# Words of w_out's tiles in the buffers of the passes' partial results, zeros through TensorE at the start, omega by one transfer

## The chip, the cores and the metric

The kernel runs on one core of a Trainium2 chip. The metric is the device time of one execution in microseconds (us). Below, TensorE is the matmul engine, DVE the vector engine, ACT the scalar engine, and SyncE the engine in whose queue (SPq) most transfers are issued, in order.

## The reference

Three stages follow each other: linear attention with random features, and two feed-forward blocks.

```python
def _attn_ref(q, k, v, omega):        # (4, 8, 576, 64) each; omega (128, 64)
    q_s, k_s = q * scale, k * scale
    def phi(x):
        h = einsum('bhsd,md->bhsm', x, omega) - sum(x * x) / 2
        return exp(h - max(h)) / sqrt(m)
    kv  = einsum('bhsm,bhsd->bhmd', phi(k_s), v)
    num = einsum('bhsm,bhmd->bhsd', phi(q_s), kv)
    return num / (phi(q_s) . sum_s phi(k_s) + 1e-6)

def _moe_ref(x, w_a, w_b, w_out):     # x (2304, 512), w_a and w_b (512, 1536), w_out (1536, 512)
    return (x @ w_a * (x @ w_b)) @ w_out

def _moe2_ref(x, w_in, w_out):        # w_in (512, 2048), w_out (2048, 512)
    h = maximum(x @ w_in, 0)
    return (h * h) @ w_out
```

The weights are 64-bit floats in memory. The kernel reads them as pairs of 32-bit words.

## The kernel before, in words

Every 64-bit weight is turned into a sum of two reduced-precision parts, high and low. `load` brings the words of one or two 128x512 pieces into a buffer named `raw` (two buffers of 8 KB per partition); `split` makes the two parts: ACT reads the upper words into `a` (L211), DVE puts the bits together in `p` in three steps (L212, L216, L220; L220 is the last reader of the words), ACT casts the high part (L226), and DVE subtracts for the low part (L227). A tile of w_a and one of w_b share a `raw` buffer (L194); a tile of w_out takes one for itself (L190).

The prologue loads omega twice (L365, L366), side by side, transposes it on TensorE (L375), and ACT writes it as OMS, OM and OMZ. The first head pair of k is loaded (L441), transposed (L465), copied to S on ACT (L468), projected with OMZ in full precision (`phi_wide`, L415), reduced on DVE for the minimum (L419) and put through the exponential on ACT (L421). The last 64 rows of all heads, the tail, go the same way in `kt_steps` after a transpose of their own (`tail_turn`, L403). Products of k's features with v are `ps_kv` (L571) and `ps_kt` (L539).

The first feed-forward block runs in passes over one block of 256 tokens (passes 0 to 5) or two (later ones). A pass of the first six covers half the hidden dimension, six tiles f; for every f there are the gate matmuls `ab` (L786) with w_a and w_b, and two units later the matmuls `y` (L811) with w_out in `outs`. Passes 0 and 1 (f 0 to 5) make w_out's tiles 0 to 5 new; passes 2 and 3 (f 6 to 11) the tiles 6 to 11. A made tile is stored as `wo_d` and loaded again later (L1597). At the end of a pass the sums in PSUM go to a tile of `ypool`: in passes 0, 1 and 4 as `y_s` (ACT, L846), then to memory (L847); in passes 2, 3 and 5 the earlier half is loaded as `y_p` (`prefetch`, L976) and added (DVE, L840). `ypool` has two buffers of 2 KB per partition with the tag `ys`; in the first 40 us they hold V2, the v of odd head pairs. Attention lanes for later batches (`SIDES`) are laid between the units. The order on each engine and queue is fixed when the program is built.

The units and their splits are driven by `load_split`, which issues a load, and by `step`, which counts units down until the split is laid out. `tc.issue_after(x)` makes the instructions of its block come after x on x's engine.

Of the kernel before, what the change touches and what calls it, by code (L numbers as in the profile page):

```python
# [8 lines left out]
F32 = mybir.dt.float32  # L9
# [35 lines left out]
def kernel(  # L45
# [13 lines left out]
    nc = tc.nc  # L59
# [122 lines left out]

    def load(*parts):


        raw = top["raw"].tile([128, 2, 512, 2], I32, tag="raw", name="raw")
# [13 lines left out]
    def split(raw, t, behind=None, apart=False, put_off=None):  # L200
# [3 lines left out]
        n = raw.shape[1]  # L204
# [3 lines left out]
        for x in (slice(0, 1), slice(1, 2)) if apart else (slice(0, n),):  # L208
            a, p, r, o = a_[:, x], p_[:, x], raw[:, x], t[:, x]
            with tc.issue_after(behind.ins) if behind else nullcontext():  # L210
                nc.scalar.activation(out=a, in_=f32(r[:, :, :, 1]), func=ACTF.Copy, scale=WORD_SCALE)  # L211
# [8 lines left out]
            nc.vector.scalar_tensor_tensor(  # L220
                out=p.bitcast(U32), in0=r[:, :, :, 0].bitcast(U32), scalar=29,
                in1=p.bitcast(U32), op0=ALU.logical_shift_right, op1=ALU.bitwise_or,
            )
# [18 lines left out]
    later_parts, later_n = [], [9]  # L242
# [114 lines left out]

    def prologue():
# [49 lines left out]
    def phi_wide(rows, dst):  # L408
# [5 lines left out]
        for x, s in enumerate(rows):  # L414
            state["proj"] = nc.tensor.matmul(  # L415
                ps[:, 2 * x:2 * x + 2].rearrange("p h m -> p (h m)"), lhsT=s,
                rhs=OMZ.rearrange("p h m -> p (h m)"), start=True, stop=True,
            )
# [7 lines left out]
    class Side:  # L426
# [28 lines left out]
        def t1_main(self):  # L455
# [60 lines left out]
    def kt_steps(b, g):  # L516
# [11 lines left out]
        st = tail_turn("k", b, g)  # L528
# [246 lines left out]
    def a_units():  # L775
# [26 lines left out]
        def outs(pi, f):  # L802
# [26 lines left out]
            if wide:  # L829
                for c in range(KC):  # L830
                    t = ypool.tile([128, 2, N], F32, tag="ys", name="y_s")
# [5 lines left out]
            for c in range(0, KC, 2):  # L837
# [6 lines left out]
                else:  # L844
                    t = ypool.tile([128, 2, N], F32, tag="ys", name="y_s")
# [125 lines left out]
        def prefetch(pi, f):  # L971
            bl, f0, f1 = PASSES[pi]
            if f0 and f == f1 - 1:
                for c in range(0, KC, 2):
                    part[pi, c] = ypool.tile([128, 2, N], F32, tag="ys", name="y_p")
# [814 lines left out]
```

## Time and profile before

| | |
|---|---|
| Time, median of 3 runs (lowest to highest) | 978.43 us (976.73 to 978.84) |
| Profiled execution, its own time | 979.28 us |
| Its span in the trace | 977.2 us |
| TensorE busy (share of the span) | 961.5 us (98%) |
| DVE busy | 728.8 us (75%) |
| ACT busy | 551.5 us (56%) |
| Chain of work that ended last | TensorE 81%, DVE 7%, transfers 5%, ACT 4% |

The span runs from the first instruction to the last; the profiled execution's own time has 2.1 us more around it. Busy time counts an engine as busy while any of its instructions is under way. Matmuls overlap each other in the pipeline, so the time from one start to the next says more of their rate than their duration does. A full-precision matmul of 256 columns shows as two records.

### The profile page before, as it was taken

To read this page: it belongs to the slowest core of one execution; us is meant where nothing else is said; L and a number is where in the kernel's file an instruction comes from. 1 tells how busy PE (TensorE), PEld (TensorE's weight loads), DVE (VectorE), ACT (ScalarE), POOL (GpSimd) and SP (SyncE) were. 2 spreads that over 40 slices of the span, in tenths; PEclk is the share of its full clock that TensorE was granted. 3 is DMA by queue.
4 is the path that set the end of the run, shared out by engine and by line. 5 is a ranking of instruction groups with operands and counts; after the bars stand their busy time and mean duration, and the time that the engine had idled before them with its cause. 6 is when DMAs were issued, how large, how long until landed. Compare 5 with 4: busy or idle time off the path is not lost.

```text
span 977.2 us, 18208 instructions
## 1 busy us (share of the span) xinstructions
PE 961.5 (98%) x6625; PEld 898.0 (92%) x6625; DVE 728.8 (75%) x1688; ACT 551.5 (56%) x1310; POOL 28.8 (3%) x54
## 2 busy tenths in 40 slices
PE   7999999999999999999999999999999999999998
PEld 6799998999998889889998888899999999999998
DVE  3888689887787865565456989789787347988794
ACT  5876566666655643253433544677676565555561
POOL 4000100000000000000000000000000000000000
PEclk9999999999999999999999999999999999999999
DMA  8656976655775365346547989246666869944301
GB/s 207 208 176 204 307 234 212 226 179 182 218 213 167 130 199 171 113 153 188 170 143 254 350 304 339 66 160 207 216 227 220 317 250 357 390 135 146 115 17 50
DMA packets 121961, 198.39 MB, mean 203 GB/s; under 512 B 28944, under 2 KB 84752, under 8 KB 119440
## 3 DMA queue, kind: packets, MB, share of 16 engines
q1 hardware_dynamic: 120336, 195.65, 60.5%
q0 software_dynamic: 1536, 1.58, 0.6%
q8 instruction: 53, 0.87, 0.4%
q14 instruction: 36, 0.29, 0.1%
HBM read 136.90 MB, written 60.29 MB: 202 GB/s over the span
## 4 chain that ended last, share of the span: by engine, by line
PE 81%; DVE 7%; DMA 5%; ACT 4%; issue 2%; SPq 0%; DVEq 0%; ACTq 0%
PE y L811 13%; PE abw L786 9%; PE oY L1478 8%; PE pY L1294 7%; PE ab L786 7%; PE oX L1478 5%; PE oW L1478 5%; PE sP L919 5%; PE pW L1294 4%; PE sR L919 3%; PE ps_n L638 3%; PE ps_kv L571 3%; PE ps_p L415 3%; PE ps_p L490 2%; DMA raw<-in_moe_w_b_dram 2%; PE ps_qt L628 2%
## 5 line engine op out<-in xcount | busy, mean ns | idle before, releaser
L786 PE MATMUL abw<-x_all,W 128*128 128x512 f32 x432 | 104.1, 392 | 0.0
L786 PEld LDWEIGHTS abw<-x_all,W 128*128 128x128 f32 x432 | 80.0, 188 | 15.7
L786 PE MATMUL ab<-x_all,W 128*128 128x256 f32 x576 | 84.9, 290 | 0.4 <-ACT W L226 0.4
L786 PEld LDWEIGHTS ab<-x_all,W 128*128 128x128 f32 x576 | 74.0, 189 | 1.7 <-ACT W L226 0.6
L811 PE MATMUL y<-g_mid,wo 128*128 128x512 f32 x288 | 75.1, 401 | 0.0
L811 PE MATMUL y<-gs,wo 128*128 128x256 f32 x432 | 66.5, 290 | 0.0
L811 PEld LDWEIGHTS y<-g_mid,wo 128*128 128x128 f32 x288 | 51.9, 188 | 10.1
L811 PEld LDWEIGHTS y<-gs,wo 128*128 128x128 f32 x432 | 56.6, 189 | 1.0 <-DVE wo L227 0.2
L1294 PE MATMUL pY<-W,M 128*128 128x384 f32 x228 | 44.1, 336 | 0.4 <-ACT F L1312 0.4
L499 ACT COPY c<-ps_p 128x256 f32<-128x256 f32 x76 | 27.7, 372 | 28.6 <-PE ps_p L490 28.1
L501 DVE CUSTOM_DVE_ANT_0 c<-ps_p,c 128x128 f32<-128x128 f32 x152 | 38.2, 285 | 7.5 <-ACT c L499 6.8
L786 PE MATMUL ab<-x,W 128*128 128x256 f32 x288 | 42.5, 288 | 0.0
L1442 ACT CAST W<-F 128x384 fp32r<-128x384 f32 x57 | 29.1, 513 | 22.9 <-PE oX L1478 11.0
L1478 PE MATMUL oX<-W 128*128 128x256 f32 x351 | 41.9, 276 | 0.0
L1478 PEld LDWEIGHTS oX<-W 128*128 128x128 f32 x351 | 40.8, 188 | 0.0
L1294 PEld LDWEIGHTS pY<-W,M 128*128 128x128 f32 x228 | 39.8, 188 | 1.0 <-ACT F L1312 0.9
L1320 ACT ACTIVATE F<-F 128x384 f32<-128x384 f32 x48 | 24.7, 518 | 26.9 <-DVE F L1315 26.7
L1478 PE MATMUL oY<-W 128*128 128x256 f32 x315 | 38.6, 277 | 0.0
L786 PEld LDWEIGHTS ab<-x,W 128*128 128x128 f32 x288 | 37.6, 191 | 0.1
L506 ACT ACTIVATE qp<-c,nm 128x128 f32<-128x128 f32 x88 | 31.0, 397 | 11.3 <-DVE nm L501 10.8
L1478 PEld LDWEIGHTS oY<-W 128*128 128x128 f32 x315 | 37.1, 188 | 0.0
L419 DVE TENSOR_REDUCE nm<-ps_p 128x4 f32<-128x512 f32 (+1 forms) x44 | 24.7, 564 | 14.9 <-PE ps_p L415 14.7
(287 smaller groups left out, 2408.7 us busy)
## 6 DMA issues: line engine op xcount, KB each, us to landing
wo<-wo_d SPq DMA_DIRECT2D x60, 512.0 KB, 3.9
s_d<-F SPq DMA_DIRECT2D x24, 768.0 KB, 4.7
tsum<-t_d SPq DMA_DIRECT2D x26, 512.0 KB, 4.0
t_d<-cut SPq DMA_DIRECT2D x40, 256.0 KB, 2.9
raw<-in_moe_w_out_dram SPq DMA_DIRECT2D x32, 256.0 KB, 5.2
raw<-in_moe_w_in_dram SPq DMA_DIRECT2D x16, 512.0 KB, 6.4
raw<-in_moe_w_a_dram SPq DMA_DIRECT2D x12, 512.0 KB, 3.8
raw<-in_moe_w_b_dram SPq DMA_DIRECT2D x12, 512.0 KB, 5.8
```

The source lines that it names most:

```text
L415: state["proj"] = nc.tensor.matmul(ps[:, 2 * x:2 * x + 2].rearrange("p h m -> p (h m)"), lhsT=s, rhs=OMZ.rearrange("p h m -> p (h m)"), st ...
L499: nc.scalar.copy(out=c, in_=ps[:, :, 1, :])
L501: nc.vector.tensor_tensor_reduce(out=c[:, x, :], in0=ps[:, x, 0, :], in1=c[:, x, :], scale=1.0, scalar=3.0e38, op0=ALU.add, op1=ALU.min, a ...
L506: nc.scalar.activation(out=dst[:, 2 * n + x, :], in_=c[:, x, :], func=ACTF.Exp, scale=-1.0, bias=nm[:, x:x + 1],)
L571: lambda h=h, j=j: nc.tensor.matmul(ps[:, h, :], lhsT=kp[:, 4 * h + j, :], rhs=V2[h][:, j] if odd else V[:, j, h, :], start=(j == j0), sto ...
L638: lambda x=x: nc.tensor.matmul(pn[:, x, :], lhsT=t["qT"][:, x % 2 * len(g) + x // 2, :], rhs=kv[:, x % 2, :], start=True, stop=True,)
L786: nc.tensor.matmul(ps, lhsT=wv[:, s_, kc, :], rhs=x[..., kc, m_, :], start=(kc == 0 and (s_, m_) == TERMS[0]), stop=(kc == KC - 1 and (s_, ...
L811: nc.tensor.matmul(y_part(pi, f, c), lhsT=wo[pi, f][:, s_, c * 128:(c + 1) * 128], rhs=g[:, m_, :],  start=(f == f0 and (wide or c % 2 == ...
L919: nc.tensor.matmul(ps[:, z], lhsT=b(z, s_, kk), rhs=a[:, kk, m_, :], start=(first and z == 0 and kk == 0 and (s_, m_) == TERMS[0]), stop=( ...
L1294: nc.tensor.matmul(ps[c][:, x, 0:TH], lhsT=w[:, s_, 128 * kk:128 * kk + 128], rhs=y[:, ai, kk, m_, :], start=((c, x) not in seen and kk == ...
L1442: ahead_of["cast"] = nc.scalar.copy(out=sop[:, 0], in_=src)
L1478: nc.tensor.matmul(tiles_of(p, t), lhsT=sops[n][:, s_, 128 * t:128 * t + 128], rhs=w[:, m_, :], start=(fresh and k == 0 and (t % 2 == 0 or ...
```

## The change

Three things are changed. First, from w_out's third tile on (`O_APART = 2`) `load` puts the words into two tiles of `ypool` with the tag `ys`, 512 words each, by two transfers, and `split` reads them in two halves, on ACT (L211 before) and in the last of the three DVE steps (L220 before). `y_stage`, by which the passes' results now get their tiles, first lays out the splits of all such tiles that are still waiting.

Second, a region of W that is not yet in use is filled with zeros, copied from OMZ, which is cleared first; V and VT are cleared after that. TensorE multiplies these zeros into a bank that nobody reads: 8 matmuls ahead of omega's transpose, 6 after it, and 4 after the transposes of the first tile of k. The first projections stand behind the last of them, and the tail's transpose behind the projections.

Third, omega comes by one transfer that reads it twice. The laying out of the first tile's parts also moves by one step (`later_n`, 9 to 10).

```diff
+    def y_stage(name):
+        while any(x[1][0] == "o" and x[1][1] >= O_APART for x in waiting):
+            split_next()
+        return ypool.tile([128, 2, N], F32, tag="ys", name=name)
     def load(*parts):
+        if parts[0][2] and parts[0][1] >= O_APART:
+            w, f, _ = parts[0]
+            raws = []
+            for z in range(2):
+                t = ypool.tile([128, 2, N], F32, tag="ys", name="rawo").rearrange("p a n -> p (a n)")
+                nc.sync.dma_start(
+                    out=i32(t), in_=w[f * 128:(f + 1) * 128, 512 * z:512 * z + 512]
+                )
+                raws.append(i32(t).rearrange("p (f w) -> p f w", w=2))
+            return raws
...
             with tc.issue_after(behind.ins) if behind else nullcontext():
-                nc.scalar.activation(out=a, in_=f32(r[:, :, :, 1]), func=ACTF.Copy, scale=WORD_SCALE)
+                for a_x, _, r in pieces:
+                    nc.scalar.activation(
+                        out=a_x, in_=f32(r[..., 1]), func=ACTF.Copy, scale=WORD_SCALE
+                    )
...
-    later_parts, later_n = [], [9]
+    later_parts, later_n = [], [10]
...
+    zero = area["W"][:, FA * 2048 - 256:FA * 2048]
+    blank = bank(7, [128, 512], "blank")[:, 0:256]
+    def fill(n):
+        for _ in range(n):
+            state["fill"] = nc.tensor.matmul(
+                blank, lhsT=zero[:, 0:128], rhs=zero, start=True, stop=True,
+            )
...
-        nc.sync.dma_start(out=om[:, 0, :], in_=omega)
-        nc.sync.dma_start(out=om[:, 1, :], in_=omega)
-        nc.vector.memset(V, 1.0)
-        nc.vector.memset(VT, 1.0)
+        nc.sync.dma_start(out=om, in_=omega.unsqueeze(1).to_broadcast([M, 2, D]))
+        nc.vector.memset(OMZ, 0.0)
+        t = nc.vector.tensor_copy(out=zero, in_=OMZ.rearrange("p a m -> p (a m)"))
+        with tc.issue_after(t.ins):
+            t = nc.vector.memset(V, 1.0)
+        with tc.issue_after(t.ins):
+            nc.vector.memset(VT, 1.0)
...
-        nc.vector.memset(OMZ, 0.0)
+        fill(8)
         ps = at_bank([128, M], "ps_om")
-        nc.tensor.transpose(ps, om.rearrange("p a d -> p (a d)"), ident)
+        with tc.issue_after(state["fill"].ins):
+            t = nc.tensor.transpose(ps, om.rearrange("p a d -> p (a d)"), ident)
+        with tc.issue_after(t.ins):
+            fill(6)
...
+        with tc.issue_after(state["fill"].ins) if "proj" not in state else nullcontext():
             for x, s in enumerate(rows):
                 state["proj"] = nc.tensor.matmul(
...
+            elif "k" in self.at:
+                with tc.issue_after(state["fill"].ins):
+                    for c in cols:
+                        t = nc.tensor.transpose(ps[:, c], nat[:, c], ident)
+                with tc.issue_after(t.ins):
+                    fill(4)
...
         yield
-        st = tail_turn("k", b, g)
+        if state["n"] < 4:
+            yield
+            with tc.issue_after(state["proj"].ins):
+                st = tail_turn("k", b, g)
+        else:
+            st = tail_turn("k", b, g)
```

The four places that took `ypool.tile(..., tag="ys", ...)` for `y_s` and `y_p` call `y_stage` instead, the one in the wide passes too.

## Rows read from the trace of the kernel before

**Rows 1.** The page: busy us (share of the span) and instructions

```profile
PE 961.5 (98%) x6625; PEld 898.0 (92%) x6625; DVE 728.8 (75%) x1688; ACT 551.5 (56%) x1310; POOL 28.8 (3%) x54
```

**Rows 2.** Waits of TensorE, whole run: us in total, times, longest us

```profile
PE ps_om L375 <- DMA om<-in_omega_dram: 3.0, 1, 3.0
```

**Rows 3.** Timeline of TensorE, 0 to 16: start us, us, engine, line, names, count

```profile
5.00 1.11 PE L465 MATMUL ps_t<-ident,kn 128*128 128x128 f32 x4 [1.54 <-DMA kn<-in_k_dram]
6.79 1.22 PE L415 MATMUL ps_p<-OMZ,S 128*128 128x256 f32 x2 [0.68 <-ACT S L468]
...
8.02 2.77 PE L415 MATMUL ps_p<-OMZ,S 128*128 128x256 f32 x6
10.58 1.06 PE L415 MATMUL ps_p<-OMZ,T 128*128 128x256 f32 x2
...
12.28 0.42 PE L463 MATMUL ps_t<-ident,qn 128*128 128x128 f32 x1
...
12.82 0.30 PE L465 MATMUL ps_t<-ident,kn 128*128 128x128 f32 x1
...
15.00 1.35 PE L415 MATMUL ps_p<-OMZ,S 128*128 128x256 f32 x5
```

**Rows 4.** Busy us of PE, PEld, DVE, ACT, POOL; clock, DMA; 40 to 180

```profile
40.00:180.00 140.00, 137.67 (x1077) 130.54 (x1076) 117.74 (x260) 91.42 (x233) 9.34 (x16) 1.00 0.72 231
```

**Rows 5.** Waits of SyncE's queue, 40 to 180; landing of L190's loads

```profile
SPq L190 <- DVE p L220: 24.2, 7, 5.7
SPq L194 <- DVE p L220: 18.4, 8, 4.5
...
DMA to landing us min/median/max: 3.4/3.9/7.7
```

**Rows 6.** Timeline of DVE, 0 to 13

```profile
0.95 0.49 DVE L369 MEMSET V<- 128x520 f32 x1
...
1.99 0.27 DVE L373 MEMSET OMZ<- 128x256 f32 x1
...
9.11 0.69 DVE L419 TENSOR_REDUCE nm<-ps_p 128x4 f32<-128x512 f32 x1 [4.25 <-PE ps_p L415]
```

**Rows 7.** Groups by form, ACT, then DVE: count | busy us, mean ns

```profile
L211 ACT ACTIVATE a<-raw 128x512 f32<-128x512 f32 x16 | 10.9, 680 | 8.6 <-DVE den L612 2.7 <-DMA raw<-in_moe_w_b_dram 2.4 <-DVE den L609 1.6
...
L1065 DVE TENSOR_TENSOR gs<-a_s,gs 128x256 fp32r<-128x256 f32 x36 | 15.1, 419 | 1.6 <-ACT gs L1065 1.2
...
L220 DVE SCALAR_TENSOR_TENSOR p<-raw,p 128x512 uint32<-128x512 uint32 x16 | 10.9, 686 | 0.2
```

**Rows 8.** Timeline of SyncE's queue, 0 to 6

```profile
1.19 0.42 SPq L366 DMA_DIRECT2D om<-in_omega_dram  x1
1.65 0.43 SPq L441 DMA_DIRECT2D kn<-in_k_dram  x1
2.13 0.77 SPq L561 DMA_DIRECT2D V<-in_v_dram  x1
```

**Rows 9.** Timeline of TensorE, from 118 on

```profile
119.51 2.99 PE L786 MATMUL ab<-x_all,W 128*128 128x256 f32 x24
```

**Rows 10.** Timeline of ACT, 0 to 15

```profile
11.54 1.14 ACT L421 ACTIVATE kp<-ps_p,nm 128x128 f32<-128x128 f32 x4 [0.57 <-DVE nm L419]
...
14.57 0.87 ACT L468 COPY S<-ps_t 128x256 f32<-128x256 f32 x2
```

**Rows 11.** Timeline of SyncE's queue, 118 to 182

```profile
137.17 1.44 SPq L847 DMA_DIRECT2D y_d<-y_s  x2
...
140.06 0.85 SPq L190 DMA_DIRECT2D raw<-in_moe_w_out_dram  x1
143.69 0.93 SPq L976 DMA_DIRECT2D y_p<-y_d  x2
```

**Rows 12.** Timeline of DVE, 120 to 180

```profile
133.85 0.68 DVE L220 SCALAR_TENSOR_TENSOR p<-raw,p 128x512 uint32<-128x512 uint32 x1
...
173.64 1.29 DVE L840 SCALAR_TENSOR_TENSOR y_p<-y,y_p 128x512 f32<-128x512 f32 x2
```

More of the change, by code (lines that the diff above doesn't have):

```diff
@@ L200, in split @@
     def split(raw, t, behind=None, apart=False, put_off=None):
-        n = raw.shape[1]
+        halves = None
+        if isinstance(raw, list):
+            halves = [(slice(256 * z, 256 * z + 256), r) for z, r in enumerate(raw)]
+        n = 1 if halves else raw.shape[1]
         a_, p_ = (
@@ L208, in split @@
         for x in (slice(0, 1), slice(1, 2)) if apart else (slice(0, n),):
-            a, p, r, o = a_[:, x], p_[:, x], raw[:, x], t[:, x]
+            a, p, o = a_[:, x], p_[:, x], t[:, x]
+            if halves:
+                pieces = [(a[:, 0, c], p[:, 0, c], r) for c, r in halves]
+            else:
+                pieces = [(a, p, raw[:, x])]
             with tc.issue_after(behind.ins) if behind else nullcontext():
-                nc.scalar.activation(out=a, in_=f32(r[:, :, :, 1]), func=ACTF.Copy, scale=WORD_SCALE)
+                for a_x, _, r in pieces:
+                    nc.scalar.activation(
+                        out=a_x, in_=f32(r[..., 1]), func=ACTF.Copy, scale=WORD_SCALE
+                    )
             nc.vector.tensor_scalar(
@@ L219, in split @@
             )
[L220 to L223, printed above, removed]
+            for _, p_x, r in pieces:
+                nc.vector.scalar_tensor_tensor(
+                    out=p_x.bitcast(U32), in0=r[..., 0].bitcast(U32), scalar=29,
+                    in1=p_x.bitcast(U32), op0=ALU.logical_shift_right, op1=ALU.bitwise_or,
+                )
             def parts(o=o, p=p):
@@ L413, in phi_wide @@
         ps = at_bank([128, n, M], "ps_p")
[L414 to L418, printed above, removed]
+        with tc.issue_after(state["fill"].ins) if "proj" not in state else nullcontext():
+            for x, s in enumerate(rows):
+                state["proj"] = nc.tensor.matmul(
+                    ps[:, 2 * x:2 * x + 2].rearrange("p h m -> p (h m)"), lhsT=s,
+                    rhs=OMZ.rearrange("p h m -> p (h m)"), start=True, stop=True,
+                )
         nc.vector.tensor_reduce(out=nm, in_=ps, axis=AXX, op=ALU.min)
@@ L830, in outs @@
                 for c in range(KC):
-                    t = ypool.tile([128, 2, N], F32, tag="ys", name="y_s")
+                    t = y_stage("y_s")
                     nc.scalar.mul(out=t, in_=yp[pi][c], mul=Y_SCALE)
@@ L844, in outs @@
                 else:
-                    t = ypool.tile([128, 2, N], F32, tag="ys", name="y_s")
+                    t = y_stage("y_s")
                     nc.scalar.mul(out=t, in_=yp[pi][c // 2], mul=Y_SCALE)
@@ L974, in prefetch @@
                 for c in range(0, KC, 2):
-                    part[pi, c] = ypool.tile([128, 2, N], F32, tag="ys", name="y_p")
+                    part[pi, c] = y_stage("y_p")
                     nc.sync.dma_start(out=part[pi, c], in_=y_cols(bl[0])[:, c:c + 2, :])
```

3 lines of the change are left out of this document (added).

## The prediction

> **What bounds the kernel now.** I read the page's busy shares first: TensorE is busy 98% of the span [rows 1], so nothing but an idle or a slow stretch of TensorE can be won, and any stall put into its in-order queue is paid in full. Next the list of what TensorE waited for: its two longest waits of the whole run are both in the first 5 us, 3.0 us for omega and 1.5 us for the first tile of k [rows 2, 3]. Then the timeline of its first 15 us [rows 3]. What to see there is not only the gaps but the spacing: six records of the projection `ps_p` start at 8.02 and the next form starts at 10.58, 0.427 us a record; the five from 15.00 on last 1.35 us together, some 0.24 a record (less the drain of the last). So TensorE runs at half its rate (1.2 instead of 2.4 GHz) until about 12.8: a transpose's duration is 0.42 at 12.28 and 0.30 at 12.82 [rows 3]. The granted clock of the page shows full rate there; I go by the spacing. Before the rise the engine had worked since 6.79, from 8.02 on without any break.
>
> For the middle of the kernel I read one window and one list. In the 140 us from 40 to 180, in which all the w_out splits that the change touches lie (the first two excepted), TensorE is idle for only 140.00 - 137.67 = 2.33 us, beside DVE at 84% [rows 4]. In the same stretch SyncE's queue stands 24.2 and 18.4 us for a `raw` buffer, that is for the last DVE operation of an earlier split [rows 5]. The queue waits; TensorE hardly does.
>
> **The start, step by step.** OMZ is cleared first, then copied to the zeros. The memset is 0.27 us and starts at 0.95 in the place of V's [rows 6]; the trace has no such copy, so I take between 0.27 (that memset) and 0.42 (a DVE operation of the same 128x256 on two inputs [rows 7]). The zeros stand at about 1.6. V's memset then ends at some 2.1 instead of 1.44, and V's load is behind it in SyncE's queue: it was issued at 2.13 [rows 8], so it keeps its place, and all loads behind it keep theirs.
>
> Omega by one transfer takes one issue of 0.42 us out of the queue, and the load of k behind it moves from 1.65 to about 1.2 [rows 8]. Its price as one issue is not in the trace; twice as many runs as one of the two halves, so between 0.42 and the 0.77 of V's load. Gain for k: 0 to 0.45 us.
>
> The 18 fills are 128x256 matmuls. Twenty-four of that form take 2.99 us at full rate, 0.12 us each [rows 9]; at half rate 0.24. Eight run from 1.6 to 3.5, omega's transpose follows (it waited until 3.02 before), six more end at about 5.2, then come the four transposes of k, which began at 5.00. While the clock is low the fills thus take the whole gain of the earlier k, and cost up to 0.3 us; four more behind the transposes cover S's copy (done just before 6.79 [rows 3]) and end about when it does. TensorE is at work without a break from 1.6.
>
> When does the clock rise? The one rise of this trace came 4.8 to 6.0 us after the work became unbroken (from 8.02, or from 6.79 if a first short break is not counted, to 12.8) [rows 3]. The same distance from 1.6 gives 6.4 to 7.6; I take 7.1, just as `ps_p` starts. Then the chain is: first four records at half of 0.427 each and 0.16 of drain, done at 8.1 (the reduce started at 9.11 [rows 6]); reduce 0.69, then four exponentials 1.14: 9.95. The other four records end at 9.1, their exponentials wait for ACT and end at 11.1 (before: 11.54 + 1.14 = 12.68 [rows 10]). The remaining products of k and v are some 0.9 us at full rate, so S is copied at 12.3 instead of 14.57, and the next projections start at 12.7 instead of 15.00: 2.3 us saved. TensorE would save 2.9 at full rate (13 records and transposes, 0.21 each); ACT's chain of exponentials keeps 0.6 of it. If the clock rises at 6, the sum is 2.7; at 8.5, about 1.2; never earlier than now, 0.3 lost. From 15 on the work is bound by TensorE, ACT and DVE, not by times of arrival, so I carry 2.3 us to the end.
>
> On the clock the Trainium skill, "TensorE: Matmul & The Clock Gate", section "Part 4: PE-mode transpose", says that transposes do not count as busy TensorE in the way that matmuls do. The kernel before cannot decide it: its only early transposes are followed by a gap. By that rule the zeros fall into pieces with transposes between, which is the second rival below. The tail's transpose of k is also put behind the first projections; it stood between two of them and cost the first reduce one record, 0.21 us at half rate, and that is in the sum above.
>
> **The places of w_out.** For ten of the twelve splits the words go to the two `ys` buffers instead of half a `raw` buffer. Each costs one more issue (0.34 us on SyncE), and two halves on DVE: 2 x 0.42 instead of 0.69 [rows 7], 0.15 us, so 1.5 us of DVE in 140, beside TensorE's work. ACT's own pass over the words is cut in two likewise, at most the same 0.15 each. I cost this at nothing: DVE has 22 us of idle in the stretch [rows 4], and if that cover were gone it would be 1.5.
>
> What it gives: w_a's and w_b's pairs no longer queue behind w_out's words, up to 24.2 + 18.4 us of SyncE's waits [rows 5]. For TensorE that is worth at most its idle 2.33 us.
>
> What it adds: both `ys` buffers make one tile of w_out, so from one such load to the next nothing overlaps: the next is issued only when the last DVE operation of the split before has read both halves, and the partial results of the passes stand in the same two buffers. The worst place is pass 2, where six w_out tiles, two stores of y and two loads of y_p meet. Before, load 8 was issued at 140.06 while the stores of y were still under way, and y_p was loaded at 143.69, thirty us ahead of its use at 173.64 [rows 11, 12]. After, load 8 waits for the stores to land and y_p for the last split. One turn is the load's 3.9 us [rows 5], ACT's 0.7 [rows 7] and the three DVE operations with what stands between them, some 2.5: 7.1. Tile 6 has its words read by 134.5 as before [rows 12], 7 by about 141; y is evicted behind that and stored until about 148 (before, store and landing took from 137.17 to at most 143.69 [rows 11]), then 8, 9, 10 and 11 at 155, 162, 169 and 176, and y_p lands at 180. The eviction that ends the pass came at 173.64 [rows 12], so the w_out lane would end the pass some 6 us late, 3 if a turn is 6.3. Queued behind these waits on SyncE are loads of q and k and the reloads of w_out. TensorE has other work then: gate matmuls of two units (each 2.99 [rows 9]) and the attention lanes. I take the lateness as covered to most of its length and set gain against loss: 0, with -2.3 and +7 as the ends.
>
> The sum: -2.3 + 0. From the profiled execution's 979.28 (span 977.2 and 2.1 around it) that is 977.0; that execution stood 0.85 above the median of 978.43, so I forecast 976.1, with 974.8 to 977.3 as its own range from the clock's rise at 6 or at 8.5.
>
> **Rivals.**
> The raw buffers pay. With w_a and w_b earlier, the idle of 40 to 180 goes: 976.1 - 2.3 = 973.8. For: the queue's 42 us of waits. Against: DVE, at 84%, takes the splits no faster.
>
> The clock does not rise earlier (the zeros, or the transposes among them, count for less than the rows suggest): 0.3 us late instead of 2.3 early, 978.7. Against: the one rise in the trace followed work that also had transposes in it, as at 12.28 [rows 3].
>
> The ys buffers become the bound, and it is slower than before. The place is pass 2 and the start of pass 3; y's matmuls of pass 3 need the banks that the eviction with y_p frees, due at 173.64. It decides as soon as that eviction is later than the work at hand covers: the two gate units are 6.0 us if they are still free to run, nothing if their own buffers wait for the same y. 180 against 173.64 is 6.4; I take 5: 976.1 + 5 = 981.1. For: single buffering where there were two. Against: TensorE's idle of 2.33 us shows that the order laid out at build time finds other work.
>
> **How the numbers follow.** Chances: forecast 0.45, raw buffers pay 0.22, no earlier rise 0.17, ys the bound 0.16. A measurement of this kernel tells about 0.2% from no change, 1.96 us, so faster means under 976.5 and slower over 980.4. Of the forecast 0.32 lies below 976.5; with 0.21 of the first rival and 0.01 of the second, faster is 0.54. Slower is 0.14 of the last rival and 0.02 of the second, 0.16. The rest, 0.30, is the same. The range reaches down to 973.4 (both gains, 2.7 and 2.3, off 978.4) and up to 980.6 (the lower half of the last rival).
>
> **What would show it.** The start is right if the spacing of `ps_p` falls to 0.22 before 8 us and the projections of 15.00 come at about 12.7; wrong if records at 0.43 still stand at 10. The single omega shows in k's issue at 1.2. The ys lane shows in SyncE's waits: those of w_a and w_b for a raw buffer shrink, and loads of w_out stand for the split before or for y's store. If TensorE's idle in the stretch of passes 2 and 3 grows by more than 2 us, the last rival holds. The forecast fails if the build lays out the attention lanes in another order, which no row here can show.

## The result and the profile after

The changed kernel takes **982.33 us** (median of 7 runs, 981.45 to 985.5) against 977.96 for the kernel before (7 runs, 975.95 to 979.28): a ratio of **1.0053, interval 1.0038 to 1.0069**. It is slower by 0.4 to 0.7%, above the range of 973.4 to 980.6. The profiled execution has a span of 980.1 us.

In every fence below, the line numbers are those of the changed kernel: L461 is the projection (L415 before), L843 the gate matmuls (L786), L199 a load of w_out's words into a `ys` buffer (`rawo`), L212 a load of w_a's or w_b's pair, L249 the DVE operation that reads a split's words last.

The page, busy us and share of the span, and the same window as [rows 4] (busy us of PE, PEld, DVE, ACT, POOL; clock, DMA):

```profile
PE 963.6 (98%) x6643; PEld 899.0 (92%) x6643; DVE 730.1 (74%) x1699; ACT 553.8 (57%) x1320; POOL 29.0 (3%) x54
```

```profile
40.00:180.00 140.00, 136.79 (x1066) 129.37 (x1065) 114.00 (x261) 90.87 (x236) 9.44 (x16) 1.00 0.64 211
```

TensorE is still the bound. Between 40 and 180 us it idles 3.2 us where it idled 2.3 [rows 4], with eleven matmuls fewer done in the stretch.

**The start** is better than forecast in this execution. TensorE's timeline of the first 18 us, after (start us, us, engine, line, names, count, idle before):

```profile
1.55 2.07 PE L393 MATMUL blank<-W 128*128 128x256 f32 x8 [1.55 <-DVE W L408]
3.42 0.41 PE L418 MATMUL ps_om<-ident,om 128*128 128x128 f32 x1
...
4.92 0.64 PE L513 MATMUL ps_t<-ident,kn 128*128 128x128 f32 x4
...
6.23 1.13 PE L461 MATMUL ps_p<-OMZ,S 128*128 128x256 f32 x4 [0.20 <-ACT S L520]
...
7.30 1.03 PE L461 MATMUL ps_p<-OMZ,S 128*128 128x256 f32 x4
...
11.59 2.42 PE L461 MATMUL ps_p<-OMZ,S 128*128 128x256 f32 x10
...
16.97 0.63 PE L517 MATMUL ps_t<-ident,kn 128*128 128x128 f32 x4 [0.80 <-DMA kn<-in_k_dram]
```

Four transposes of k take 0.64 us where they took 1.11, and four projections 1.13 where six took 2.77 [rows 3]: TensorE is at 2.4 GHz by 4.9 us, where before it was by 12.8. (The granted clock of the profile reads 1.00 in all of these stretches, before and after, so this goes by durations and spacing, as in the prediction.) The next projections start at 11.59 instead of 15.00. But then the four transposes at 16.97 stand 0.80 us for a tile of k: the start has caught up with its loads.

The clock does not rise as early in every execution with these 18 zeros. In yp_pool, a run below with the same start, the first four projections take 1.50 us in place of 1.13, so the rise falls among them, and the next projections come 0.8 us later than in the change:

```profile
6.66 1.50 PE L461 MATMUL ps_p<-OMZ,S 128*128 128x256 f32 x4
...
12.39 2.43 PE L461 MATMUL ps_p<-OMZ,S 128*128 128x256 f32 x10
```

**Pass 2** runs much as laid down in the prediction. SyncE's queue from 118 us on (`x2` are the two halves of a tile; the `x3` are the second half of tile 8 and both of tile 9), and the eviction with y_p on DVE:

```profile
133.04 0.82 SPq L199 DMA_DIRECT2D rawo<-in_moe_w_out_dram  x2
...
145.41 6.24 SPq L199 DMA_DIRECT2D rawo<-in_moe_w_out_dram  x3
...
161.46 0.80 SPq L199 DMA_DIRECT2D rawo<-in_moe_w_out_dram  x2
...
168.60 0.80 SPq L199 DMA_DIRECT2D rawo<-in_moe_w_out_dram  x2
...
175.02 0.89 SPq L1033 DMA_DIRECT2D y_p<-y_d  x2
176.00 0.42 SPq L1654 DMA_DIRECT2D wo<-wo_d  x1
```

```profile
178.45 0.69 DVE L897 SCALAR_TENSOR_TENSOR y_p<-y,y_p 128x512 f32<-128x512 f32 x1
```

From 161.46 to 168.60 is one turn of the single pair of buffers, 7.14 us. y_p is loaded at 175.02 instead of 143.69 [rows 11], and the eviction of the pass begins at 178.45 instead of 173.64 [rows 12], 4.8 us late. Behind y_p's wait in SyncE's queue stands the reload of w_out for pass 3, issued at 176.00. TensorE's waits from 140 to 190 us (us in total, times, longest), and SyncE's from 40 to 180:

```profile
PE y L868 <- DMA wo<-wo_d: 1.4, 1, 1.4
PE ps_xt L763 <- DVE xh L670: 0.9, 1, 0.9
PE ps_p L461 <- ACT T L450: 0.6, 1, 0.6
PE ps_nt L751 <- ACT qT L747: 0.5, 1, 0.5
```

```profile
SPq L199 <- DVE p L249: 25.3, 8, 4.9
SPq L212 <- DVE p L249: 21.4, 6, 7.1
```

The four waits of TensorE are the stretch's whole idle time, 3.4 us. Before, the same stretch had 1.1 us of it:

```profile
140.00:190.00 50.00, 48.94 (x389) 46.05 (x389) 43.65 (x127) 32.71 (x87) 3.51 (x6) 1.00 0.74 243
```

It has thus grown by 2.3 us. More than 2 us of it in passes 2 and 3 was the prediction's sign for its last rival. SyncE's two waits for a buffer, which the change might have been thought to end, are 25.3 and 21.4 us instead of 24.2 and 18.4 [rows 5]: they did not shrink.

### The profile page after: what moved, and what is told of

It reads as the page before. It is cut to its first block, busy times and chain, and to the rows that moved or that the text cites. A ratio compares the mean times of both kernels' runs of the same rounds, so it can differ in the third digit from the quotient of the medians.

```text
span 980.1 us, 18274 instructions
## 1 busy us (share of the span) xinstructions
PE 963.6 (98%) x6643; PEld 899.0 (92%) x6643; DVE 730.1 (74%) x1699; ACT 553.8 (57%) x1320; POOL 29.0 (3%) x54
## 4 chain that ended last, share of the span: by engine, by line
PE 82%; DVE 6%; DMA 5%; ACT 3%; issue 1%; SPq 1%; DVEq 0%; ACTq 0%
PE y L868 14%; PE abw L843 9%; PE pY L1351 8%; PE ab L843 8%; PE oY L1535 7%; PE oX L1535 5%; PE sP L976 5%; PE oW L1535 4%; PE pW L1351 4%; PE sR L976 3%; PE ps_n L695 3%; PE ps_kv L628 2%; DMA t_d<-cut 2%; PE pX L1351 2%; PE ps_p L461 2%; PE ps_p L542 2%
## 5 line engine op out<-in xcount | busy, mean ns | idle before, releaser
L843 PE MATMUL abw<-x_all,W 128*128 128x512 f32 x432 | 104.2, 392 | 0.0
L843 PEld LDWEIGHTS abw<-x_all,W 128*128 128x128 f32 x432 | 80.0, 188 | 15.8
L843 PE MATMUL ab<-x_all,W 128*128 128x256 f32 x576 | 84.1, 289 | 0.0
L843 PEld LDWEIGHTS ab<-x_all,W 128*128 128x128 f32 x576 | 73.7, 189 | 0.9 <-ACT W L255 0.2
L843 PE MATMUL ab<-x,W 128*128 128x256 f32 x288 | 43.5, 289 | 0.0
L843 PEld LDWEIGHTS ab<-x,W 128*128 128x128 f32 x288 | 37.9, 190 | 0.0
L558 ACT ACTIVATE qp<-c,nm 128x128 f32<-128x128 f32 x88 | 30.9, 397 | 11.3 <-DVE nm L553 10.5
L695 PEld LDWEIGHTS ps_n<-kvr,qT 128*128 128x128 f32 x256 | 32.0, 191 | 4.1 <-ACT qT L690 2.4
```

The costliest lines, as they stand in the source:

```text
L558: nc.scalar.activation(out=dst[:, 2 * n + x, :], in_=c[:, x, :], func=ACTF.Exp, scale=-1.0, bias=nm[:, x:x + 1],)
L695: lambda x=x: nc.tensor.matmul(pn[:, x, :], lhsT=t["qT"][:, x % 2 * len(g) + x // 2, :], rhs=kv[:, x % 2, :], start=True, stop=True,)
L843: nc.tensor.matmul(ps, lhsT=wv[:, s_, kc, :], rhs=x[..., kc, m_, :], start=(kc == 0 and (s_, m_) == TERMS[0]), stop=(kc == KC - 1 and (s_, ...
```

## The experiments

Theory S at the outset: the start gains and w_out's places cost, and both add. Its rival, R, put the loss on the order of the lanes that the moved start brings with it. Later runs ask what of the places costs, and where the start's gain goes. All medians are given beside the kernel before on the same chip.

### One half of the change at a time

start_only keeps the change's start, with w_out as before:

```diff
-    O_APART = 2
+    O_APART = 99
```

> The changed kernel without its new places for w_out: the words of all tiles go to the raw buffers, as before; zeros, single omega transfer and order of the start are kept. Theory S (the start wins what the trace of the changed kernel shows at 20 us, 2.4, and the w_out places lose all the rest): faster than before by 2.4, that is about 975.5, ratio 0.9975. Rival R (the moved start makes the build lay out the later lanes in another order, and it is that order that loses between 200 and 280): 978 to 980, ratio 1.000 to 1.002.

Measured: 977.4 (11 runs) against 977.85, 0.9998 [0.9989, 1.0007]. Neither expectation is met. The premise of rival R fails too: from 40 to 300 us all of TensorE's 1996 matmuls stand in the order of the kernel before. start_again is the same kernel once more.

> The start alone once more, for a second profile. At 15 us it should lead by about 3 again (the clock rises near 4.8). If the loss of 2.8 between 240 and 285 is of its nature, it comes again; if it is chance, it is smaller or elsewhere.

Measured: 978.33, and a span of 976.2, as in the first. The start alone is thus worth 0.4 us and not distinguishable from nothing, though its projections stand at 12.02 and 11.52 in the two, instead of 15.00 [rows 3]. before_again is the kernel before once more.

> The kernel before once more, for a second profile. It tells how much of a lag between two profiles is chance. If the stretch from 240 to 285 was lucky in the first profile (stores of t_d landing early), this one lags it there by 1 to 3 us; if the shifted start loses there by its nature, this one agrees with the first within 0.3.

Measured: 976.77, span 974.9. It corrects a number that the prediction rests on: in this execution the projections of [rows 3] come at 14.00, not 15.00. The transposes ahead of them take 0.28 us each from 11.27 on, so the clock had risen by then, against 12.8 in the first profile. So 1.0 of the 3.4 us between [rows 3] and the profile after is a late start of the kernel before. On the stretch from 240 to 285 us it agrees with the first profile to about 0.3 us (its matmuls compared with the first profile's, one by one in order). start_only loses 3.0 us there against that profile, start_again 1.7: a loss that comes again, though not in full.

ys_only has the places, and the start as before:

```diff
-        nc.sync.dma_start(out=om, in_=omega.unsqueeze(1).to_broadcast([M, 2, D]))
+        nc.sync.dma_start(out=om[:, 0, :], in_=omega)
+        nc.sync.dma_start(out=om[:, 1, :], in_=omega)
...
-        fill(8)
...
-            fill(6)
...
```

(the rest of the start goes back in the same way, `later_n` too)

> The kernel before with the new places for w_out alone; the start is that of before. Theory S: slower than before by 4.4 + 2.4 = 6.8, about 984.7, ratio 1.007, and the lag against before grows at 75 to 95, 140 to 185 and 200 to 280. Rival R: slower by no more than what is lost up to 185, about 4, ratio 1.004, with no further loss between 200 and 280.

Measured: 985.03, 1.0074 [1.0061, 1.0086]: 7.2 us slower, as theory S had it. **The places are the loss.**

### Which tiles

early_four uses the places for tiles 2 to 5, late_six for 6 to 11 (which meet the stores of y and y_p in pass 2); the start is the change's in both:

```diff
-    O_APART = 2
+    O_APART = range(2, 6)
```

(in the two comparisons, `in` for `>=`), and

```diff
-    O_APART = 2
+    O_APART = 6
```

> The changed kernel with the new places for w_out's tiles 2 to 5 alone (pass 0); tiles 6 to 11 stay in the raw buffers, so y's stores and the loads of y_p share their buffers with nothing. Theory S: only the loss of 75 to 95 stays: 975.5 + 1.9 = 977.4, ratio 0.9995. Rival: if the loss between 200 and 280 stays too, about 980.

> The changed kernel with the new places for w_out's tiles 6 to 11 alone (passes 1 and 2); tiles 2 to 5 stay in the raw buffers. Theory S: the loss of 75 to 95 (1.6 to 2.2) is gone and the losses of passes 2 and 3 and after stay: about 980.5, ratio 1.0025. Rival: if the loss is that of the early tiles, about 977.

Measured: early_four 980.79, 1.0029 [1.0019, 1.0038]; late_six 981.89, 1.0045 [1.0031, 1.006]; both beside start_only's 977.4. The four early tiles cost 3.4 us, the six late ones 4.5, together more than the whole change's 4.9. Theory S had 1.9 for the early tiles and missed; early_four's time is near that of its rival, about 980. Busy time in two stretches, as in [rows 4], of start_only, early_four and late_six in turn:

```profile
75.00:100.00 25.00, 24.96 (x204) 24.28 (x203) 21.47 (x49) 16.49 (x42) 3.54 (x7) 1.00 0.66 219
...
140.00:190.00 50.00, 49.11 (x393) 46.45 (x392) 43.92 (x128) 31.98 (x85) 3.50 (x6) 1.00 0.75 244
```

```profile
75.00:100.00 25.00, 24.24 (x187) 23.00 (x188) 21.14 (x51) 15.07 (x39) 3.39 (x6) 1.00 0.64 212
...
140.00:190.00 50.00, 47.77 (x378) 44.88 (x377) 43.28 (x126) 32.64 (x87) 3.51 (x6) 1.00 0.74 240
```

```profile
75.00:100.00 25.00, 24.96 (x200) 24.17 (x199) 21.64 (x47) 16.41 (x40) 2.33 (x4) 1.00 0.69 237
...
140.00:190.00 50.00, 46.55 (x360) 43.14 (x361) 42.34 (x127) 31.46 (x88) 3.49 (x6) 1.00 0.57 189
```

TensorE's idle from 75 to 100 us, where no partial result stands in the way, goes from 0.04 to 0.76 us with the early tiles and not with the late ones. From 140 to 190 the late tiles take it from 0.9 to 3.45, as much as the whole change shows there; the early ones to 2.2. The number of matmuls done tells the same: 189 and 365 in the whole change, 204 and 393 in start_only.

### Queues

yp_pool issues y_p's two loads from GpSimd's queue, so that the reload of w_out does not stand behind them:

```diff
-                    nc.sync.dma_start(out=part[pi, c], in_=y_cols(bl[0])[:, c:c + 2, :])
+                    nc.gpsimd.dma_start(out=part[pi, c], in_=y_cols(bl[0])[:, c:c + 2, :])
```

> The changed kernel with the loads of y_p issued from GpSimd's queue instead of SyncE's. Theory (the reload of w_out for pass 3 stands in SyncE's queue behind the loads of y_p, which wait for the last split): the wait of y for that reload, 1.4 us near 180, goes, the time falls by about that, to 981. Rival (it is y_p itself, late, that holds the eviction and so the banks): the wait moves to the eviction, and the time stays at 982.3.

Measured: 982.65, 1.0047 [1.0028, 1.0065]: both expected times lie in the interval. TensorE's wait of 1.4 us for the reload is gone; what stands in its place, from 165 to 190 us, is

```profile
PE y L868 <- DVE y_p L897: 0.4, 1, 0.4
```

The time is not told apart from the change's: 1 us less in one wait is inside the interval. pool_queue moves the words of w_out to GpSimd's queue as well:

```diff
-                nc.sync.dma_start(
+                nc.gpsimd.dma_start(
                     out=i32(t), in_=w[f * 128:(f + 1) * 128, 512 * z:512 * z + 512]
```

> The whole change, with the loads of w_out's words into the ys buffers and the loads of y_p issued from GpSimd's queue, so that nothing on SyncE's queue stands behind a wait for a ys buffer. If what the places cost is what stands behind these waits on SyncE (loads of q and k, the reload of wo), most of the 5 us between after and start_only goes: 977.5 to 979.5. If it is the order in which the lanes stand on the engines, and the single pair of buffers itself, the time stays at 981 to 983.

Measured: 990.62, 1.0129 [1.0108, 1.015], far above both expectations. GpSimd's queue carries the tails of k, q and v, and these now stand behind the waits (40 to 190 us):

```profile
POOL rawo L199 <- DVE p L249: 29.2, 3, 10.6
POOL rawo L199 <- DVE xh L670: 25.4, 1, 25.4
```

So the waiting was not lifted by another queue, only moved to one with other work in it. By which of these waits it became 8 us worse was not followed further.

### The places or the halves

halves_in_raw takes away the places, and with them `y_stage`'s early laying out of the waiting splits, which no run tells apart from the places. The words still come in two loads and are read in two halves by ACT and DVE, but they lie in a half of a `raw` buffer, and the partial results have the `ys` buffers for themselves. The start is the change's.

```diff
-        while any(x[1][0] == "o" and x[1][1] >= O_APART for x in waiting):
-            split_next()
...
+            raw = top["raw"].tile([128, 2, 512, 2], I32, tag="raw", name="raw")
...
-                t = ypool.tile([128, 2, N], F32, tag="ys", name="rawo").rearrange("p a n -> p (a n)")
+                t = raw[:, 0, 256 * z:256 * z + 256]
...
```

> The whole change but the places: w_out's tiles from the third on are loaded in two halves and read in two halves by ACT and DVE as in after, but the words stay in half a raw buffer, and the partial results of the passes have the ys buffers for themselves as in before. The start is after's, with 18 fills. If the single pair of buffers is what costs (each load waits for the split before, for y's stores, and y_p for the last split), this runs as start_only does, 977.4, plus at most the 1.5 us of DVE: 977.4 to 978.9. If the halves and the other order in which the lanes then stand on the engines are the cost, it runs as after: 981 to 983.

Measured: 976.9 (12 runs), 0.9989 [0.9977, 1.0002]: 5.4 us below the change, near the expectation of the single pair (977.4 to 978.9). Another order of the lanes comes with the halves too: of start_only's 1996 matmuls between 40 and 300 us, 1752 are found in the same order in this kernel, 1754 in early_four, 1802 in late_six and 1723 in the change. early_four and late_six, whose order is no newer than this one, lose 3.4 and 4.5 us; this one loses nothing. It isn't the very order of the change. halves_again is the same kernel once more.

> One more look at halves_in_raw. Its first profile showed TensorE at a wait of 1.3 us for the third tile of k at 17 us and a granted clock of 0.85 and 0.50 in the two stretches of 5 us from 15. If that belongs to the early start of this kernel it comes again; if it belongs to that execution, the granted clock stays 1.00 and the span is some 974.5.

Measured: 976.73, span 975.0. Busy time by stage, of the change and then of halves_again:

```profile
75.00:100.00 25.00, 24.24 (x189) 22.87 (x188) 21.18 (x50) 16.01 (x41) 3.12 (x6) 1.00 0.63 217
140.00:190.00 50.00, 46.60 (x365) 43.49 (x364) 42.71 (x127) 31.75 (x90) 3.01 (x6) 1.00 0.55 186
190.00:260.00 70.00, 68.45 (x556) 65.18 (x555) 56.51 (x212) 46.07 (x140) 3.99 (x7) 1.00 0.63 192
```

```profile
75.00:100.00 25.00, 24.95 (x200) 23.83 (x199) 21.77 (x51) 16.87 (x44) 2.92 (x6) 1.00 0.70 227
140.00:190.00 50.00, 48.34 (x385) 45.80 (x384) 44.15 (x131) 32.07 (x89) 3.49 (x6) 1.00 0.73 239
190.00:260.00 70.00, 69.77 (x575) 67.15 (x574) 59.06 (x229) 48.69 (x154) 3.49 (x6) 1.00 0.64 195
```

Idle time of TensorE is 0.76, 3.40 and 1.55 us against 0.05, 1.66 and 0.23, so 3.8 of the 5.1 us between the two spans. DVE, ACT and the DMA engines do less in the change's stretches too: none of them has become the bound. And w_a's and w_b's loads, which were to be freed, wait less where w_out stays beside them: 17.7 us in halves_again from 40 to 190, 21.4 in the change.

### How many zeros

three_fills is start_only with one zero product in each of the three places, 3 instead of 18:

```diff
-        fill(8)
+        fill(1)
...
-            fill(6)
+            fill(1)
...
-                    fill(4)
+                    fill(1)
```

> The start alone with three zero matmuls in all (one at each place) instead of eighteen; order and single omega transfer kept. Theory (the unbroken work of the zeros brings the clock's rise forward): the rise falls back to about 12, and the lead at 15 us falls from 3.0 to 0.4 or less. Rival (the earlier k and the moved tail's transpose make most of the lead): the lead stays at 2 or more.

> The same kernel as three_fills, beside three_short on the same chip: 975.7 (975.0 to 976.4) again. A profile that loses over 1 us behind 20 us against the first one would say that such losses belong to an execution and not to the kernel.

Measured: three_fills 975.71 (10 runs), **0.9982 [0.9970, 0.9994]**, and three_again, the same kernel, 976.13 (12 runs), 0.9984 [0.9973, 0.9996]. Both are faster than the kernel before, with a later rise of the clock than the change has. TensorE's first microseconds:

```profile
6.18 2.04 PE L461 MATMUL ps_p<-OMZ,S 128*128 128x256 f32 x4 [0.46 <-ACT S L520]
...
8.18 1.03 PE L461 MATMUL ps_p<-OMZ,S 128*128 128x256 f32 x4
...
12.45 2.42 PE L461 MATMUL ps_p<-OMZ,S 128*128 128x256 f32 x10
```

The rise falls between the first four projections and the next, at about 8 us, and the projections of 11.59 come at 12.45; in three_again they come at 13.15. So the lead over [rows 3] stayed near 2 us (2.6 and 1.9), as the rival had it, but the clock rose well ahead of the 12 us of the theory. No run has the new order of the start without any zeros, so what the three zeros give of these 2 us, and what the earlier k and the single transfer of omega, is not told apart.

three_again also lost more behind 20 us than three_fills did: its span is 2.6 us longer, and 0.7 of that is the start. By its own expectation such losses belong to an execution. A single wait of one profile is to be read with that in mind.

Compared with start_only, all other instructions stand in the same order on every engine. start_only's projections come at 12.02 (11.52 in start_again), 0.4 to 0.9 us ahead of three_fills, and its median is 1.7 behind. Its start leads TensorE to the third tile of k before it has landed, and there the lead ends: the transposes of that tile stand at 16.84 in start_only, 16.83 in start_again and 16.87 in three_fills. Behind that start_only loses more. Theory F for this loss: 15 products and 15 weight loads more move each later fetch of TensorE's instructions against the work, onto transfers that the lanes wait for. Three kernels vary the number and the work apart. short_fills has 18 fills of 8 columns:

```diff
-                blank, lhsT=zero[:, 0:128], rhs=zero, start=True, stop=True,
+                blank[:, 0:8], lhsT=zero[:, 0:128], rhs=zero[:, 0:8], start=True, stop=True,
```

> The start alone with its 18 fills, but each of 8 columns instead of 256: as many instructions on TensorE as in start_only, hardly any of their work. start_only (18 fills) ran 977.4, three_fills 975.7, and the two differ in nothing but 15 zero products ahead of the first projections. Theory F, the fetches of TensorE's instructions: 15 products and their 15 weight loads more move each later fetch to an earlier place in the work, where it falls beside stores of t_d and a load of w_b that the attention lanes wait for. Then the number of instructions counts, not their work: TensorE loses 0.8 us at 55 to 63 and over 1 us each near 246 and 267, as in start_only, and the time is 977.4 (976.7 to 978.1). Rival C, the early rise of the clock itself sets the lanes against their transfers: with fills this short the clock rises as late as in three_fills (about 8 us), and the time is 975.7 (975.0 to 976.4).

Measured: 979.1 (12 runs), 1.001 [0.9998, 1.0021], above both expectations. Its timeline:

```profile
6.48 2.07 PE L461 MATMUL ps_p<-OMZ,S 128*128 128x256 f32 x4
...
14.76 1.56 PE L461 MATMUL ps_p<-OMZ,S 128*128 128x256 f32 x6
```

The clock rises late, as in the kernel before (a transpose of 0.42 us at 12.40, one of 0.28 at 12.83), and not at about 8 us as both sides had assumed; the projections come at 14.76. So the change's start without its rise is no gain. The rise is what start_only has over it: 2.7 to 3.2 us at the projections, 1.7 in the median, with intervals that overlap. nine_wide has 9 fills of 512 columns:

```diff
-    blank = bank(7, [128, 512], "blank")[:, 0:256]
+    blank = bank(7, [128, 512], "blank").rearrange("p (a n) -> p a n", a=2)
...
-                blank, lhsT=zero[:, 0:128], rhs=zero, start=True, stop=True,
+                blank, lhsT=zero[:, 0:128], rhs=zero.unsqueeze(1).to_broadcast([128, 2, 256]), start=True, stop=True,
...
-        fill(8)
+        fill(4)
...
```

(and 3 and 2 in place of 6 and 4)

> The start alone with 9 fills of 512 columns in the place of 18 of 256: the same work on TensorE, so the clock should rise as early as in start_only (about 5 us), with 9 products and 9 weight loads fewer. Theory F: what counts is where the fetches fall; they come some 1.1 us later against the work than in start_only and 0.4 us earlier than in three_fills, so the long landings of t_d near 243 and 261 go at least in part, and the time is 975.2 to 976.5. Rival C: the early rise is what the later lanes lose by, 977.4 (976.8 to 978.0).

Measured: 976.3 (12 runs), 0.9985 [0.9974, 0.9996], with the early rise (projections at 11.90). That is in theory F's range and below rival C's, though the interval (975.2 to 977.4 us) reaches into the latter. three_short has one long fill and else short ones in each group, 18 in all:

```diff
-        for _ in range(n):
+        for x in range(n):
+            c = 256 if x == 0 else 8
             state["fill"] = nc.tensor.matmul(
-                blank, lhsT=zero[:, 0:128], rhs=zero, start=True, stop=True,
+                blank[:, 0:c], lhsT=zero[:, 0:128], rhs=zero[:, 0:c], start=True, stop=True,
```

> The start alone with 18 fills in three groups as in start_only, of which only the first of each group has 256 columns and the other 15 have 8. TensorE has three_fills' long zeros and start_only's number of instructions; every other instruction on every engine stands as in both. Theory F (the number of instructions moves the fetches onto transfers that the lanes wait for): 977.4 (976.6 to 978.1), with the projections near 12.4 as in three_fills and 1 to 2 us lost behind 20 us against three_fills. Rival (the 15 instructions do not matter; what start_only and nine_wide lost behind 20 us goes with how early the lanes start, or with the one execution that was profiled): 975.7 (975.0 to 976.4). If the clock rises later than about 8 us, the distance of the next projections from 12.45 is to be taken off first.

Measured: 979.42 (12 runs), 1.0013 [1.0001, 1.0025]. Its projections come at 13.65, 0.5 us behind three_again, its time is 3.3 behind. With the 1.2 us to 12.45 taken off, as the expectation has it, that is 978.2, just above theory F's 978.1 and far from the rival's 975.7. So in this order of the lanes the 15 short instructions cost something that is not the work of the zeros. Where three_short loses: TensorE's waits for the exponential L558 from 40 to 300 us, of three_short and then of three_again,

```profile
PE ps_qt L685 <- ACT qp L558: 3.2, 2, 1.7
```

```profile
PE ps_qt L685 <- ACT qp L558: 0.3, 1, 0.3
```

and ACT's timeline where the longest of them arises, again three_short and then three_again:

```profile
249.08 0.41 ACT L330 CAST cut<-full 128x256 fp32r<-128x256 f32 x1 [1.48 <-DMA t_d<-cut]
```

```profile
247.62 0.39 ACT L330 CAST cut<-full 128x256 fp32r<-128x256 f32 x1
```

The cast waits until an earlier store of `t_d` has landed and frees its buffer; the exponential stands behind the cast on ACT, and TensorE behind the exponential. start_only shows the same wait with 2.7 us and start_again with 1.5, the kernels with 3 and 9 fills 0 to 0.3. The DMA view of that moment, three_short (243 to 248 us) and three_again (243 to 250): packets, MB and share of 16 engines by queue, and median us to landing by transfer.

```profile
q8 instruction: 1, 0.02, 2.5%
...
t_d<-cut SPq DMA_DIRECT2D x2, 256.0 KB, 4.8
```

```profile
q8 instruction: 1, 0.02, 1.0%
...
t_d<-cut SPq DMA_DIRECT2D x3, 256.0 KB, 3.1
```

In three_short one fetch of TensorE's instructions takes 2.5% of 16 engines for 5 us, 2.0 us of one engine, and the stores beside it land in 4.8 us; in three_again 1.0% of 7 us, 1.1, and the stores land in 3.1. This fits theory F. It does not settle it: short_fills has the same number of instructions and shows only 0.7 us of this wait, and nine_wide lost 2.2 us in its profile near 151 us, where the words of w_b landed 7.6 us after their issue with no such fetch beside them. Shown is that the 15 instructions cost in this order: 979.42 against 976.13 with the same long zeros, and 977.4 for start_only, which starts earlier than both. short_fills is 3.0 to 3.4 us behind the two kernels with 3 fills, with projections that come 1.6 to 2.3 later. Not shown is that the fetches are the way.

three_after has the whole change with 3 fills; halves_three has the halves in the raw buffers with 3 fills:

> The whole change, with 3 fills instead of 18. If the places of w_out cost 7.2 us whatever the start does (ys_only against before), the time is 975.7 + 7.2 = 982.9, the same as after within 0.7. If the whole change carries a cost of its 15 further fills as start_only does, it is after's 982.3 less 1.7, 980.6.

Measured: 983.7 (6 runs), 1.0057 [1.0035, 1.008]. The first expectation holds, the second does not. Beside three_fills and three_again the places cost 7.6 to 8.0 us, as in ys_only; beside start_only they cost 4.9. So 3 zeros in place of 18, which gain 1.3 to 1.7 us without the places, gain nothing beside them.

> halves_in_raw with 3 fills in place of 18: w_out's words in two halves but in the raw buffers, and the start of three_fills. If halves cost nothing of themselves, this runs as three_fills does, 975.9 (975.0 to 976.8). If halves_in_raw's 976.9 hides a cost of halves beside a start that lost 2.6 us between 15 and 25 us (granted clock 0.50 at 20 to 25 in its profile), it stands about 1 above three_fills. If the halves even help (ACT's and DVE's passes are shorter), it stands below 975.

Measured: 976.68 (12 runs), 0.9984 [0.9976, 0.9993], the ratio of three_fills. The halves cost nothing. Nor do 15 further zeros in this order of the lanes: halves_in_raw has 18 and took 976.9. Between 240 and 285 us, where start_only and start_again lose 3.0 and 1.7 us, halves_again loses 0.1 by the same count. The price of the 15 instructions is thus one of start_only's order, and no general one. Of all versions three_fills, nine_wide and halves_three are the ones below the kernel before, by 0.15 to 0.18%.

## Why the prediction was wrong

**What bounds the kernel**: right. TensorE stayed at 98%, and the stalls that the change put into its queue were paid.

**The start: mechanism right, its size a matter of the execution, and carried on too far.** The zeros stand at 1.5 us (forecast 1.6), k's load is issued at 1.25 (1.2), the load of V behind a moved memset at 2.27 (2.13 kept). In the change's profile the clock rose by 4.9 instead of 7.1, and the projections came at 11.59 instead of 12.7. In yp_pool, with the same start, the rise came behind 6.66 and the projections at 12.39. So the forecast lies at the late end of what this start does, and one rise, on which it rested [rows 3], could not tell the spread. The second rival, that the zeros or the transposes among them count for less, does not hold: the clock rose earlier than before in each profile with the 18 long zeros, in spite of omega's transpose at 3.42. The Trainium skill, "TensorE: Matmul & The Clock Gate", section "Part 4: PE-mode transpose", has it that transposes do not count as busy TensorE in the same way; this is no test of that sentence, since zeros stood on both sides of the transpose.

Then two things took the gain back. The first is a sentence of mine: "From 15 on the work is bound by TensorE, ACT and DVE, not by times of arrival". At 16.97 TensorE waits 0.80 us for k. The second I had no term for: in start_only's order the later lanes lose more with 15 instructions more at the start, as three_short shows. And the base was one execution with a late rise: before_again stood 1.0 us earlier at the same point. Of the 2.3 us that I carried to the end, start_only's median has 0.45.

**The places: the timeline right, the step "covered to most of its length ... 0" wrong.** Tiles 9 to 11, y_p's load and the eviction come nearly as forecast (a turn of 7.14 us for 7.1; y_p's load issued at 175.02 for 176; the eviction 4.8 us late for some 6; the reload of w_out behind y_p's wait, "queued behind these waits ... the reloads of w_out"). I set this lateness at nothing, because the idle of 2.3 us [rows 4] showed that the order laid out at build time finds other work. The runs show that the cover fell short: of the waits from 140 to 190 us one is for the reload, and three are in attention chains. My reading is that the same gate matmuls also cover the attention lanes, so that what is drawn ahead for the one is missing for the other; no run isolates this. The term measured +4.9 (with the change's start), +7.2 (with the start of before) and 7.6 to 8.0 (with 3 zeros), where I had put 0 and +7 as the upper end.

**The first rival, the raw buffers pay** (0.22), fell: SyncE's waits did not shrink, and TensorE's idle time from 40 to 180 us, which was to go, grew from 2.3 to 3.2 us. **The last rival, the ys buffers become the bound** (0.16), comes nearest, 981.1 for 982.3. Its mechanism is the one that halves_in_raw shows. Its place is only half right: late_six has 4.5 us, but the four early tiles, which meet no partial result, cost 3.4 on their own. What costs there goes with the pair too, one tile of w_out at a time where two `raw` buffers let the next load run ahead: with the halves in `raw` the idle time from 75 to 100 us is gone. Why the whole costs less than the sum of the two parts, and why the places cost 2 to 3 us less beside start_only than beside the other two starts, the runs do not tell in full; a part is that the change shows 0.2 us of the wait for L558 that start_only has at 2.7.

**The sentence on the lay-out** ("fails if the build lays out the attention lanes in another order") named a thing that happened. A new order is not enough for a loss: halves_in_raw has one as well and loses nothing. That the change's own order has no part in its loss is not shown.

## What to carry to other kernels

Moving words from buffers with room for two tiles to a pair with room for one cost 5 to 8 us here, although TensorE seemed to have other work: it had idled only 2.3 us in 140. Before setting a lateness at nothing, say which other waits the same cover already hides. And a start that gains 3 us at 12 us is worth what the next load lets it keep. Try the smallest form of it first: 3 zero products did as well here as 18 or better.

## What was not expected of the hardware

**After an early rise the clock can fall again.** In one profile of halves_in_raw TensorE waited for the third tile of k at 17 us longer than in the change, after the early rise, and the granted clock (third column from the right) fell:

```profile
PE ps_t L517 <- DMA kn<-in_k_dram: 1.3, 1, 1.3
```

```profile
15.00:20.00 5.00, 3.71 (x26) 3.51 (x27) 0.84 (x4) 3.39 (x10) 0.00 (x0) 0.85 1.08 238
20.00:25.00 5.00, 5.00 (x18) 4.24 (x18) 3.98 (x7) 2.22 (x7) 2.32 (x4) 0.50 0.31 81
25.00:30.00 5.00, 4.65 (x30) 3.91 (x29) 3.54 (x8) 4.02 (x12) 0.00 (x0) 0.97 0.47 131
```

From 20 to 25 us it is at 0.50, which is 1.2 GHz, and 18 matmuls are done where halves_again, with a wait of 0.4 us and a granted clock of 1.00, does 23. In steps of 1 us the granted clock is 0.75 from 18 to 19 and 0.50 from there to 25, with TensorE at work all the time. The two profiles of this one kernel differ by 2.3 us of span (977.3 and 975.0). early_four waited the same 1.3 us at that place and kept 1.00, so the wait alone does not decide it.

**Executions of one kernel start at different times.** The rise of the clock in the kernel before came at 12.8 us in one profile and by 11.3 in another. With 3 zeros it came at about 8 in three_fills, at about 9 in three_again and at about 11 in three_after, which has the same start; with 18 by 4.9 in the change and behind 6.66 in yp_pool. The projections behind it moved by up to 1.5 us. A gain of 2 us that is read from one profile of a start can hold half of that as chance.

**A few more instructions at the start can have a price far behind it.** 15 products of 8 columns, most of them where TensorE stood idle otherwise, made three_short 3.3 us slower than three_again, with 0.5 of it at the start. With w_out's halves in `raw` and another order of the lanes, 15 products of 256 columns cost nothing (976.9 against 976.68). The cause is open.
